# The head of a linear-attention and two-MLP kernel: one load in longer pieces, one pair's rests loaded alone, and a laid-down order between the head's stages

## The chip, the cores and the metric

The kernel runs on one core of a Trainium2 chip. The metric is the device time of one execution in microseconds (us); lower is better. Three runs of the kernel before gave a median of 1557.27 us.

## What is computed

```python
kv  = einsum('bhsd,bhse->bhde', k, v)          # q, k, v: 8 x 8 x 576 x 64, float32
out = einsum('bhsd,bhde->bhse', q, kv)
a   = out / sqrt(mean(out * out, -1) + 1e-6) * g_norm
x   = a.transpose(0, 2, 1, 3).reshape(4608, 512)
h   = x @ moe_w_in                             # 512 x 2048
g   = where(h >= 1, h, where(h <= -1, 0, (h + 1)**2 / 4))
x   = g @ moe_w_out                            # 2048 x 512
h   = x @ moe2_w_in;  r = maximum(h, 0);  out = (r * r) @ moe2_w_out
```

The weights arrive in 64-bit floats and are narrowed on the chip.

## The kernel before

The work goes in three parts: linear attention for eight batches of eight heads, the first MLP and the second. The first MLP's batches 0 to 6 run block by block (16 hidden blocks each), with the attention of the next batch hooked in between; the rest runs in a seven-product form afterwards. The change and the prediction are about the first 75 us only, in which batch 0's attention, the first weights' narrowing and the first MLP blocks overlap.

**Batch 0's attention.** The heads are taken in four pairs (hp 0 to 3). `load_first` starts the loads: of each pair k, v and q as tiles of 128 x 512 on SP's queue, and the last 64 positions of all eight heads (the rests, tiles kvr0 and qr0) on ACT's queue, behind them two copies of g_norm (gvec). `kv_stage` multiplies k by v on TensorE (pkv) and copies the two diagonal blocks to kv0; `t_first` transposes q (pt) and copies it to qT; `o_first` multiplies them (po), takes squares into y on ScalarE and a scaled copy into o, one half of it on VectorE; `r_first` sums the squares over a head (pr), takes Ln and Exp on ScalarE and finishes the norm on VectorE (lines 518, 521 and 522: `newton` and `norm`). Its result t is split into a high and a low part of one input chunk of the MLP: x1_0_0 to x1_0_3, one for each pair, the low part at line 229 on VectorE.

**The weights.** `split_w` takes one block of one weight matrix: a pass on ScalarE (line 267), two on VectorE (lines 269 and 270), a high part by ScalarE (line 216), a low part by VectorE (line 184). Names: w1_0_5 is block 5 of w_in, w1_1_5 block 5 of w_out, d and raw alike.

**The first MLP blocks.** `h_stage` makes hidden block f in PSUM (ph1_0_f, 12 matmuls of 512 columns), ScalarE takes the activation (u1_0_f), and VectorE clamps it at line 706, the last reading of that PSUM bank. Blocks 2 to 5 of batch 0 use the banks acc0 to acc3, in which `out_stage` then gathers the four output sums acc1_0_0 to acc1_0_3:

```python
        pool, tag = (ps_h, "h")
        if (L, b) == (1, 0) and 2 <= f < WAVE:
            pool, tag = (ps_a, f"acc{f - 2}")
```

So acc1_0_3 can begin when the clamp of block 5 has read acc3.

**What sets the order.** The stages are written down by slot numbers (`attention_first`, `SPLITS`, `WARMS`; `keep_warm` puts filler matmuls, pwarm, between them), in slot order, but a scheduling layer places the instructions on each engine's queue by its own costs. `tc.high_priority()` and `tc.issue_after(...)` steer it. Each engine then takes its queue strictly in order.

Of the kernel before, what the change touches and what calls it, by code (L numbers as in the profile page):

```python
# [9 lines left out]
F32 = mybir.dt.float32  # L10
# [66 lines left out]
def linear_attention_rms_two_mlps(  # L77
# [29 lines left out]
    WAVE = 6  # L107
    WHOLE = ((1, 0), (1, 1))
    WARMS = ((0, 5), (6, 5), (8, 3), (12, 4), (14, 3), (20, 3), (26, 3))
    SPLITS = (10, 15, 24, 29, 32, 33)  # L110

    const = ctx.enter_context(tc.tile_pool(name="const", bufs=1))
    wp = ctx.enter_context(tc.tile_pool(name="wp", bufs=1))
# [89 lines left out]
    def engine(op, phase):  # L203
        return engines[next(turns[op][min(phase, 2)])]

    def scaled(e, dst, src, scale):
        if e is nc.scalar:
            e.activation(dst, src, AF.Copy, scale=scale)
        elif e is nc.vector:
            e.tensor_scalar_mul(dst, src, scale)  # L210
        else:
            e.tensor_scalar(dst, src, scale, 0.0, op0=ALU.mult, op1=ALU.add)

    def copy(e, dst, src):
        if e is nc.scalar:
# [11 lines left out]
    def split(t, src, op, phase):  # L227
        hi = copy(engine(op + "_hi", phase), t[:, 0, :], src)
        lo = engine(op + "_lo", phase).tensor_tensor(  # L229
            t[:, 1, :], src, t[:, 0, :].bitcast(F32), ALU.subtract  # L230
        )
        return hi, lo
# [172 lines left out]
    def load_kv(b, hp):  # L405
        h0 = 2 * hp
        if b > 0:

            r = rests[turn[b, hp] % len(rests)]
            kvr[b, hp] = (r[:, 0], r[:, 1])  # L410
        for n, src in enumerate((k, v)):
            pool, tag = (ep, "e") if (b, hp) == (0, NP - 1) else (st, "st")
            t = pool.tile([P, TB], F32, tag=tag, name=f"{'kv'[n]}_{b}_{hp}")
            rows = src[b, h0 : h0 + 2, :TB, :].rearrange("h (p r) d -> p h r d", r=MR)
            if n == 0:

                t = t.rearrange("p (r h d) -> p r h d", h=2, r=MR)
                nc.sync.dma_start(t, rows.rearrange("p h r d -> p r h d"))
            else:
                t = t.rearrange("p (h r d) -> p h r d", h=2, r=MR)  # L420
                nc.sync.dma_start(t, rows)
            kvm.setdefault((b, hp), []).append(t)
            if b > 0:
                rest = src[b, h0 : h0 + 2, TB:, :].rearrange("h p d -> p h d")
                nc.sync.dma_start(kvr[b, hp][n][:REM], rest)
# [14 lines left out]
    def load_first():  # L440


        left = wp.tile([REM, 2, H, D], F32, tag="w0_7", name="kvr0")
        qr = wp.tile([REM, H, D], F32, tag="w1_6", name="qr0")
        for hp in range(NP):
            load_kv(0, hp)
            heads = slice(2 * hp, 2 * hp + 2)
            kvr[0, hp] = (left[:, 0, heads, :], left[:, 1, heads, :])
            pool, tag = (ep, "e") if hp == NP - 1 else (st, "st")
            t = pool.tile([P, TB], F32, tag=tag, name=f"q_0_{hp}")  # L450
            t = t.rearrange("p (c h d) -> p c h d", h=2, c=MR)
            rows = q[0, 2 * hp : 2 * hp + 2, :TB, :].rearrange("h (p c) d -> p c h d", p=P)
            nc.sync.dma_start(t, rows)
            qs[0, hp] = [t[:, c] for c in range(MR)] + [qr[:, heads, :]]
            if hp == 1:
                for f in range(2):
                    load_w(1, f, 0)
            if hp == 0:
                for d, src in ((left[:, 0], k), (left[:, 1], v), (qr, q)):
                    nc.scalar.dma_start(d, src[0, :, TB:, :].rearrange("h p d -> p h d"))  # L460
                for j in range(2):
                    nc.scalar.dma_start(
                        gvec[j * D : (j + 1) * D, :], g_norm.rearrange("(d o) -> d o", o=1)
                    )

    def kv_stage(b, *hps):
        ps = bank(b, f"pkv_{b}_{hps[0]}")
        for n, hp in enumerate(hps):
            kt, vt = kvm.pop((b, hp))
            r = kvr.pop((b, hp))  # L470


            for c in range(MR + 1):
                for j in range(2):
                    s = slice(j * D, (j + 1) * D)
                    d = slice(n * P + j * D, n * P + (j + 1) * D)
                    lhs, rhs = (kt[:, c, j], vt[:, j, c, :]) if c < MR else (r[0][:, j], r[1][:, j])
                    nc.tensor.matmul(ps[s, d], lhs, rhs, start=c == 0, stop=c == MR)  # L478
        for n, hp in enumerate(hps):
            for j in range(2):  # L480
                s = slice(j * D, (j + 1) * D)
                d = slice(n * P + j * D, n * P + (j + 1) * D)
                if b == 0:
                    copy(engine("kv_hi", b), kv0[s, hp, s], ps[s, d])
                    continue
                if (b, hp) in WHOLE:
                    copy(engine("kv_hi", b), kvw[s, hp % 2, s], ps[s, d])
                    continue
                t = kvbd[turn[b, hp] % len(kvbd)]
                copy(engine("kv_hi", b), t[s, 0, s], ps[s, d])  # L490
                nc.vector.tensor_tensor(t[s, 1, s], ps[s, d], t[s, 0, s].bitcast(F32), ALU.subtract)

    def t_first(hp):
        qT = scratch(hp, "qT")
        q5 = qs[0, hp]
        for half in range(2):
            ps = bank(0, f"pt_0_{hp}_{half}")
            for c in range(2):
                nc.tensor.transpose(ps[:, c * P : (c + 1) * P], q5[2 * half + c], ident)
            rest = slice(half * (REM // 2), (half + 1) * (REM // 2))  # L500
            nc.tensor.transpose(ps[:, 2 * P : U], q5[MR][rest], ident[rest, rest])
            copy(engine("q_hi", 0), qT[:, half], ps[:, :U])
        hl[0, hp] = qT

    def o_first(hp):
        qT = hl.pop((0, hp))
        y, o = scratch(hp, "y"), scratch(hp, "o")
        for half in range(2):
            ps = bank(0, f"po_0_{hp}_{half}")
            nc.tensor.matmul(ps[:, :U], kv0[:, hp, :], qT[:, half], start=True, stop=True)  # L510
            nc.scalar.activation(y[:, half], ps[:, :U], AF.Square)
            scaled(engine("o", 0), o[:, half], ps[:, :U], gvec)
        og[0, hp] = (y, o)

# [2 lines left out]

    def norm(t, y, o):  # L520
        nc.vector.scalar_tensor_tensor(t, t, -3.0, y, op0=ALU.add, op1=ALU.mult)
        nc.vector.tensor_tensor(t, o, t, ALU.mult)

    marks = []

    def r_first(hp):
        y, o = og.pop((0, hp))
        t = scratch(hp, "t")
        ms = []
        for half in range(2):  # L530
            ps = bank(0, f"pr_0_{hp}_{half}")
            m = ps[:, :U]
            nc.tensor.matmul(m, ones.bitcast(F32), y[:, half], start=True, stop=True)  # L533
            nc.scalar.activation(y[:, half], m, AF.Ln, bias=lnb, scale=LN_SCALE)
            ms.append(m)
        nc.scalar.activation(y, y, AF.Exp, bias=expb, scale=-0.5)
        square(engine("y", 0), t, y)
        for half in range(2):
            newton(t[:, half], ms[half])
        norm(t, y, o)  # L540
        n = TB // 2
        rem = xrem[0][:, hp, :].rearrange("p (h r) -> p h r", h=2)
        nc.gpsimd.tensor_copy(rem, t[:, :, n:])
        x = xs[1, 0][hp].rearrange("p a (h n) -> p a h n", h=2)
        marks.append(split(x, t[:, :, :n], "x", 0))


    def t_stage(b, hp):
# [86 lines left out]
    def attention_first():  # L635

        slots = {}

        def at(s, f, *a):
            slots.setdefault(s, []).append((f, a))  # L640

        at(0, begin, 0)
        for hp in range(NP):
            at(6 * hp, kv_stage, 0, hp)
            at(6 * hp, t_first, hp)
            at(6 * hp + 8, o_first, hp)
            at(6 * hp + 13, r_first, hp)
        return slots
# [520 lines left out]
    nc.gpsimd.memset(kvw, 0.0)  # L1169
    first = attention_first()  # L1170
    for s, n in WARMS:
        first[s].append((keep_warm, (n,)))
    order = ((0, 0), (1, 0), (2, 0), (3, 0), (4, 0), (0, 1), (1, 1), (5, 0), (2, 1))
    for i, (f, w) in enumerate(order):
        if i < 5:
            first.setdefault(SPLITS[i], []).append((split_w, (1, f, w)))
        else:
            first.setdefault(SPLITS[-1] + 1, []).append((split_later, (1, f, w)))
    for s in sorted(first):
        for f, a in first[s]:  # L1180
            if f in (o_first, r_first):
                with tc.high_priority():
                    f(*a)
            else:
                f(*a)
# [102 lines left out]
```

## Time and profile before

| | |
|---|---|
| median of three runs | 1557.27 us (1557.17 to 1559.74) |
| the profiled execution | 1557.11 us |
| its span, first to last instruction | 1555.3 us |
| TensorE busy | 1546.2 us, 99% |
| VectorE busy | 1133.4 us, 73% |
| ScalarE busy | 973.7 us, 63% |
| chain that ended last | TensorE 97% |

PE is TensorE, DVE is VectorE, ACT is ScalarE; POOL and SP are the two others, of which SP issues most loads. The chain of waits is followed back from the last instruction. A line of the timeline or of the chain gives the start and the length in us, then engine, line of the kernel, operation, and output and input by the program's names without their numbers.

### The profile page before, as it was taken

What the parts mean: (1) busy time and instruction counts of PE and PEld (TensorE: products, weight loads), DVE (VectorE), ACT (ScalarE), POOL (GpSimd) and SP (SyncE); (2) the same over time, 40 slices, a digit from 0 to 9 for tenths busy, and PEclk for the clock granted to TensorE, in tenths of its full rate; (3) what the DMA queues carried; (4) which work ended last, traced back from release to release, by engine and by line L of the source; (5) the groups of instructions that cost most, each with busy time, mean ns of one, the idle gap of its engine ahead of it and who ended that gap; (6) DMA issues with size and microseconds to landing.
All of it is one profiled execution on the core that took longest, in us unless ns stands there. A gap on an engine that the chain in (4) does not pass through costs nothing.

```text
span 1555.3 us, 22355 instructions
## 1 busy us (share of the span) xinstructions
PE 1546.2 (99%) x7729; PEld 1283.6 (83%) x7729; DVE 1133.4 (73%) x2000; ACT 973.7 (63%) x1833; POOL 20.4 (1%) x38
## 2 busy tenths in 40 slices
PE   9999999999999999999999999999999999999999
PEld 5787888888888888888888888888888888888898
DVE  6986886877877776754587558778965596568666
ACT  5977766767666676665565466456646663565374
POOL 0000000000000000000000000000000000000000
PEclk9999999999999999999999999999999999999999
DMA  9666899996878967935676877696876676877796
GB/s 290 194 217 187 274 315 277 309 314 196 275 246 243 281 207 228 295 99 169 196 245 192 224 219 245 194 250 191 258 228 204 203 239 197 242 248 223 214 389 250
DMA packets 327520, 368.23 MB, mean 237 GB/s; under 512 B 196976, under 2 KB 222576, under 8 KB 327408
## 3 DMA queue, kind: packets, MB, share of 16 engines
q1 hardware_dynamic: 295360, 308.60, 66.9%
q10 hardware_dynamic: 32048, 58.20, 9.9%
q8 instruction: 61, 1.00, 0.3%
q14 instruction: 51, 0.42, 0.1%
HBM read 282.59 MB, written 84.15 MB: 236 GB/s over the span
## 4 chain that ended last, share of the span: by engine, by line
PE 97%; ACT 1%; DVE 1%; DMA 1%; issue 0%; DVEq 0%; ACTq 0%
PE po L877 27%; PE ph L877 27%; PE acc L237 19%; PE ph L237 18%; PE po L237 1%; PE pkv L478 1%; PE pr L600 1%; PE pwarm L1150 1%; DMA wf<-wsd 1%; ACT raw L267 0%; ACT w L216 0%; PE pr L533 0%; ACT u L704 0%; DVE t L518 0%; DVE w L184 0%; PE po L510 0%
## 5 line engine op out<-in xcount | busy, mean ns | idle before, releaser
L877 PE MATMUL ph<-x,ws 128*128 128x512 f32 (+1 forms) x2016 | 422.4, 371 | 0.0
L877 PEld LDWEIGHTS ph<-x,ws 128*128 128x128 f32 x2016 | 355.9, 188 | 65.5
L877 PE MATMUL po<-t,ws 128*128 128x512 f32 x1680 | 381.6, 389 | 0.0
L877 PEld LDWEIGHTS po<-t,ws 128*128 128x128 f32 x1680 | 315.4, 188 | 65.4
L237 PE MATMUL ph<-x,w 128*128 128x512 f32 x1344 | 329.3, 392 | 1.3 <-ACT w L216 0.6
L237 PEld LDWEIGHTS ph<-x,w 128*128 128x128 f32 x1344 | 248.8, 188 | 54.0 <-ACT w L216 1.4
L806 DVE TENSOR_TENSOR t<-g,t 128x512 fp32r<-128x512 f32 (+1 forms) x288 | 183.2, 641 | 91.2 <-ACT t L216 84.2
L216 ACT CAST t<-g 128x512 fp32r<-128x512 f32 (+1 forms) x288 | 165.7, 585 | 97.2 <-DVE t L806 50.4
L237 PE MATMUL acc<-gs,w 128*128 128x512 f32 x696 | 173.0, 392 | 1.5 <-DVE u L706 1.5
L237 PE MATMUL acc<-gs,wt 128*128 128x512 f32 x648 | 157.9, 391 | 0.0
L237 PEld LDWEIGHTS acc<-gs,w 128*128 128x128 f32 x696 | 128.6, 188 | 27.8 <-DVE u L706 2.0
L934 DVE TENSOR_TENSOR h<-ph,e 128x512 f32<-128x512 f32 (+1 forms) x144 | 92.7, 645 | 67.4 <-PE ph L877 59.9
L237 PEld LDWEIGHTS acc<-gs,wt 128*128 128x128 f32 x648 | 120.1, 188 | 24.3
L704 ACT ACTIVATE u<-ph,halfb 128x512 f32<-128x512 f32 x112 | 77.3, 690 | 88.7 <-PE ph L237 86.3
L706 DVE SCALAR_TENSOR_TENSOR u<-u,ph 128x512 f32<-128x512 f32 x112 | 76.3, 681 | 54.2 <-ACT u L223 53.8
L941 ACT ACTIVATE h<-h 128x512 f32<-128x512 f32 (+1 forms) x120 | 70.3, 586 | 61.8 <-DVE h L934 57.1
L927 DVE TENSOR_TENSOR e<-ph,e 128x512 f32<-128x512 f32 (+1 forms) x96 | 60.9, 643 | 48.4 <-PE ph L877 47.4
L216 ACT CAST gs<-u 128x512 fp32r<-128x512 f32 x112 | 69.7, 622 | 38.4 <-DVE u L706 35.8
L229 DVE TENSOR_TENSOR gs<-u,gs 128x512 fp32r<-128x512 f32 x112 | 76.8, 686 | 21.7 <-ACT gs L216 21.2
L216 ACT CAST x<-xr 128x512 fp32r<-128x512 f32 (+1 forms) x84 | 49.0, 586 | 40.5 <-DVE xr L857 19.4
L942 ACT ACTIVATE g<-h 128x512 f32<-128x512 f32 (+1 forms) x120 | 70.7, 589 | 3.2
L223 ACT ACTIVATE u<-u 128x512 f32<-128x512 f32 x112 | 70.8, 632 | 1.5 <-ACT u L704 0.6
(134 smaller groups left out, 1531.8 us busy)
## 6 DMA issues: line engine op xcount, KB each, us to landing
ws<-wsd SPq DMA_DIRECT2D x336, 512.0 KB, 4.4
wsd<-s ACTq DMA_DIRECT2D x96, 512.0 KB, 4.9
wt<-wsd SPq DMA_DIRECT2D x54, 512.0 KB, 5.6
raw<-in_moe_w_in_dram SPq DMA_DIRECT2D x32, 512.0 KB, 6.0
raw<-in_moe_w_out_dram SPq DMA_DIRECT2D x32, 512.0 KB, 6.4
xr<-x1d SPq DMA_DIRECT2D x36, 256.0 KB, 4.9
out_dram<-ov SPq DMA_DIRECT2D x142, 64.0 KB, 3.7
wsd<-w SPq DMA_DIRECT2D x17, 512.0 KB, 5.0
```

The costliest lines, as they stand in the source:

```text
L216: return e.copy(dst, src)
L223: e.activation(dst, src, AF.Square)
L229: lo = engine(op + "_lo", phase).tensor_tensor(t[:, 1, :], src, t[:, 0, :].bitcast(F32), ALU.subtract)
L237: nc.tensor.matmul(dst, wt(a), xt(c), start=first and n == 0, stop=last and n == 2)
L704: nc.scalar.activation(u, ps, AF.Relu, bias=halfb, scale=0.5)
L706: nc.vector.scalar_tensor_tensor(u, u, 1.0, ps, op0=ALU.min, op1=ALU.max)
L806: engine2(op + "_lo").tensor_tensor(t[:, 1, :], src, t[:, 0, :].bitcast(F32), ALU.subtract)
L877: nc.tensor.matmul(ps, wt(a), xt(c), start=first and n == 0 and i == 0, stop=last and n == len(lhs) - 1 and i == 2, skip_group_check=True,)
L927: nc.vector.tensor_tensor(e[i, p], bank, e[i, 1], ALU.add)
L934: nc.vector.tensor_tensor(h, bank, add, ALU.add)
L941: nc.scalar.activation(u, h, AF.Relu)
L942: nc.scalar.activation(g, u, AF.Square)
```

## The change

Four edits, all for batch 0 and the first weights. k of batch 0 is loaded as v is, four positions of 64 values in one piece of 1 KB, and `kv_stage` reads it in that layout. The rests of pair 0 (two heads) get transfers of their own, and those of the other six heads follow in three more; gvec comes after these. `SPLITS` moves three of the first narrowing steps to later slots, and pairs 2 and 3 begin eight slots later. And an order is laid down: the first five narrowing steps behind a Ln and an o of certain pairs; products and transposes of pairs 2 and 3 behind the norm of the pair two before and the sum of squares of the pair before; products of pair 1 behind the transposes of pair 0.

```diff
-    SPLITS = (10, 15, 24, 29, 32, 33)
+    SPLITS = (14, 20, 26, 29, 32, 33)
...
-            if n == 0:
+            if n == 0 and b > 0:
 
                 t = t.rearrange("p (r h d) -> p r h d", h=2, r=MR)
                 nc.sync.dma_start(t, rows.rearrange("p h r d -> p r h d"))
...
-            if hp == 0:
-                for d, src in ((left[:, 0], k), (left[:, 1], v), (qr, q)):
-                    nc.scalar.dma_start(d, src[0, :, TB:, :].rearrange("h p d -> p h d"))
+            part = (slice(0, 2), slice(2, H))[min(hp, 1)]
+            for d, src in ((left[:, 0], k), (left[:, 1], v), (qr, q)) if hp < 2 else ():
+                rows = src[0, part, TB:, :].rearrange("h p d -> p h d")
+                nc.scalar.dma_start(d[:, part, :], rows)
+            if hp == 1:
                 for j in range(2):
                     nc.scalar.dma_start(
                         gvec[j * D : (j + 1) * D, :], g_norm.rearrange("(d o) -> d o", o=1)
                     )
...
-                    lhs, rhs = (kt[:, c, j], vt[:, j, c, :]) if c < MR else (r[0][:, j], r[1][:, j])
+                    lhs, rhs = (kt[:, j, c] if b == 0 else kt[:, c, j], vt[:, j, c, :]) if c < MR else (r[0][:, j], r[1][:, j])
...
         for hp in range(NP):
-            at(6 * hp, kv_stage, 0, hp)
-            at(6 * hp, t_first, hp)
+            at(6 * hp + 8 * (hp > 1), kv_stage, 0, hp)
+            at(6 * hp + 8 * (hp > 1), t_first, hp)
             at(6 * hp + 8, o_first, hp)
             at(6 * hp + 13, r_first, hp)
...
+    scales, logs, splits = [], [], []
     for s in sorted(first):
         for f, a in first[s]:
             if f in (o_first, r_first):
                 with tc.high_priority():
+                    r = f(*a)
+                (logs if f is r_first else scales).append(r)
+            elif f is split_w and len(splits) < 5:
+                splits.append(a)
+                i = (0, 1, 2, 2, 3)[len(splits) - 1]
+                with tc.issue_after(logs[i].ins), tc.issue_after(scales[i].ins):
+                    f(*a)
+            elif f in (t_first, kv_stage) and a[-1] > 1:
+                with tc.issue_after(normed[a[-1] - 2].ins), tc.issue_after(summed[a[-1] - 1].ins):
+                    f(*a)
+            elif f is t_first:
+                turned = f(*a)
+            elif f is kv_stage and a[1] > 0:
+                with tc.issue_after(turned.ins):
                     f(*a)
             else:
                 f(*a)
```

The helpers return their last instruction for this: `t_first` its last transpose, `o_first` its scaled copy (`scales`), `r_first` its last Ln (`logs`), `norm` its last multiplication (`normed`), and `summed` holds the last sum of squares. Line numbers of the changed kernel are a little higher: the clamp of line 706 is at 712, `kv_stage`'s product of 478 at 480, pt at 501 and 503, po at 513, pr at 537, pwarm at 1156.

The built order shows the change in three places. TensorE's queue behind the products of pair 1, before:

```order
L510 MATMUL po_0_0_0_284<-qT_0_0_235,kv0_126 128x288
L510 MATMUL po_0_0_1_288<-qT_0_0_235,kv0_126 128x288
L533 MATMUL pr_0_0_0_333<-y_0_0_282,ones_121 128x288
L499 MATMUL pt_0_1_0_266<-ident_120,q_0_1_149 128x128 x2
L533 MATMUL pr_0_0_1_336<-y_0_0_282,ones_121 128x288
L501 MATMUL pt_0_1_0_266<-ident_120,qr0_133 128x32
```

and in the change:

```order
L501 MATMUL pt_0_1_0_269<-ident_120,q_0_1_147 128x128
L513 MATMUL po_0_0_0_287<-qT_0_0_238,kv0_126 128x288
L513 MATMUL po_0_0_1_291<-qT_0_0_238,kv0_126 128x288
L501 MATMUL pt_0_1_0_269<-ident_120,q_0_1_147 128x128
L503 MATMUL pt_0_1_0_269<-ident_120,qr0_133 128x32
L501 MATMUL pt_0_1_1_274<-ident_120,q_0_1_147 128x128 x2
L503 MATMUL pt_0_1_1_274<-ident_120,qr0_133 128x32
L1156 LDWEIGHTS warm_188
L1156 MATMUL pwarm_295<-warm_188 128x512
L1156 LDWEIGHTS warm_188
L1156 MATMUL pwarm_295<-warm_188 128x512
L537 MATMUL pr_0_0_1_308<-y_0_0_285,ones_121 128x288
```

All six transposes of pair 1 and two filler matmuls now come ahead of the first reduction of pair 0; two more fillers and the reduction of the other half follow.

VectorE's queue up to the clamp of block 5 (u1_0_5), before:

```order
L269 TENSOR_SCALAR d1_1_5_677<-raw1_1_5_520 128x512
L706 SCALAR_TENSOR_TENSOR u1_0_3_696<-u1_0_3_696,ph1_0_3_683 128x512
L270 SCALAR_TENSOR_TENSOR d1_1_5_677<-raw1_1_5_520,d1_1_5_677 128x512
L706 SCALAR_TENSOR_TENSOR u1_0_4_780<-u1_0_4_780,ph1_0_4_767 128x512
L184 TENSOR_TENSOR w1_1_5_680<-d1_1_5_677,w1_1_5_680 128x2x256
L706 SCALAR_TENSOR_TENSOR u1_0_5_817<-u1_0_5_817,ph1_0_5_804 128x512
```

and in the change, the last twelve rows:

```order
L270 SCALAR_TENSOR_TENSOR d1_0_8_668<-raw1_0_8_619,d1_0_8_668 128x512
L270 SCALAR_TENSOR_TENSOR d1_1_6_764<-raw1_1_6_593,d1_1_6_764 128x512
L269 TENSOR_SCALAR d1_1_7_800<-raw1_1_7_635 128x512
L184 TENSOR_TENSOR w1_0_8_671<-d1_0_8_668,w1_0_8_671 128x2x256
L269 TENSOR_SCALAR d1_0_9_727<-raw1_0_9_665 128x512
L270 SCALAR_TENSOR_TENSOR d1_1_7_800<-raw1_1_7_635,d1_1_7_800 128x512
L270 SCALAR_TENSOR_TENSOR d1_0_9_727<-raw1_0_9_665,d1_0_9_727 128x512
L184 TENSOR_TENSOR w1_1_6_767<-d1_1_6_764,w1_1_6_767 128x2x256
L184 TENSOR_TENSOR w1_1_7_803<-d1_1_7_800,w1_1_7_803 128x2x256
L184 TENSOR_TENSOR w1_0_9_730<-d1_0_9_727,w1_0_9_730 128x2x256
L269 TENSOR_SCALAR d1_0_10_791<-raw1_0_10_724 128x512
L712 SCALAR_TENSOR_TENSOR u1_0_5_820<-u1_0_5_820,ph1_0_5_807 128x512
```

The narrowing of blocks 6 to 9 has moved ahead of that clamp. The low part of x1_0_3 is VectorE's 62nd row in both; the clamp is 34 instructions behind it before and 56 in the change.

TensorE's queue up to the output sum acc1_0_3, before:

```order
L237 MATMUL acc1_0_1_849<-gs1_0_0_587,w1_1_0_494 128x512 x3
L237 MATMUL acc1_0_1_849<-gs1_0_1_625,w1_1_1_501 128x512
L237 MATMUL acc1_0_2_850<-gs1_0_0_587,w1_1_0_494 128x512 x3
L237 MATMUL acc1_0_1_849<-gs1_0_1_625,w1_1_1_501 128x512 x2
L237 MATMUL acc1_0_2_850<-gs1_0_1_625,w1_1_1_501 128x512 x3
L237 MATMUL acc1_0_3_851<-gs1_0_0_587,w1_1_0_494 128x512 x3
```

and in the change:

```order
L574 MATMUL po_1_1_0_824<-qT_1_1_748,kvw_218 128x288
L574 MATMUL po_1_1_1_837<-qT_1_1_748,kvw_218 128x288
L237 MATMUL ph1_0_7_979<-x1_0_0_220,w1_0_7_625 128x512 x2
L237 MATMUL acc1_0_2_853<-gs1_0_0_590,w1_1_0_497 128x512 x3
L237 MATMUL acc1_0_2_853<-gs1_0_1_628,w1_1_1_504 128x512 x3
L237 MATMUL acc1_0_2_853<-gs1_0_2_674,w1_1_2_518 128x512 x3
L606 MATMUL pr_1_1_0_953<-wk0_1_1_746,ones_121 128x288
L606 MATMUL pr_1_1_1_956<-wk0_1_1_746,ones_121 128x288
L237 MATMUL ph1_0_7_979<-x1_0_0_220,w1_0_7_625 128x512
L237 MATMUL ph1_0_7_979<-x1_0_1_221,w1_0_7_625 128x512 x3
L237 MATMUL ph1_0_7_979<-x1_0_2_222,w1_0_7_625 128x512 x3
L237 MATMUL ph1_0_7_979<-x1_0_3_223,w1_0_7_625 128x512 x3
```

after which its next row is the first of acc1_0_3. Hidden block 7, the po and pr of batch 1's pair 1 and a third term of each output sum stand ahead of it now.

## Rows read from the trace of the kernel before

**Rows 1.** Waits of TensorE, 0 to 125 us: total us, times, longest us.
```profile
PE acc L237 <- DVE u L706: 1.5, 1, 1.5
...
PE pr L533 <- DVE t L518: 0.9, 1, 0.9
PE ph L237 <- ACT w L216: 0.6, 2, 0.4
PE ph L237 <- DVE kv L218: 0.4, 1, 0.4
```

**Rows 2.** Waits of TensorE, 125 to 1556 us.
```profile
PE po L237 <- DVE qT L559: 0.3, 1, 0.3
```

**Rows 3.** Timeline of VectorE: start us, length us, engine, line, operation.
```profile
10.60 0.15 DVE L1163 TENSOR_SCALAR gvec<-gvec 128x1 f32<-128x1 f32 x1
...
16.90 0.52 DVE L210 TENSOR_SCALAR o<-po,gvec 128x288 f32<-128x288 f32 x1 [0.98 <-ACT y L511]
...
39.50 0.68 DVE L229 TENSOR_TENSOR x<-t,x 128x512 fp32r<-128x512 f32 x1
40.10 0.75 DVE L269 TENSOR_SCALAR d<-raw 128x512 int32<-128x512 int32 x2
...
59.43 0.69 DVE L706 SCALAR_TENSOR_TENSOR u<-u,ph 128x512 f32<-128x512 f32 x1 [0.23 <-ACT u L223]
```

**Rows 4.** Windows: us, busy of PE, PEld, DVE, ACT, POOL, PEclk, DMA share, GB/s.
```profile
5.00:10.00 5.00, 5.00 (x38) 2.33 (x36) 0.26 (x1) 0.00 (x0) 0.00 (x0) 1.00 1.19 284
...
25.00:30.00 5.00, 4.57 (x20) 2.81 (x19) 4.21 (x11) 3.35 (x7) 0.51 (x1) 1.00 1.05 397
```

**Rows 5.** Chain of waits, first 15 us: start us, length us, what.
```profile
1.19 4.88 PE pwarm L1150 x11
...
9.31 0.22 PE pt L499 x2
...
10.25 0.88 PE pkv L478 x20
11.13 1.17 PE po L510 x4
...
13.28 0.49 PE pr L533 x2
...
14.49 0.75 PE pwarm L1150 x3
```

**Rows 6.** Timeline of ScalarE and its DMA issues (ACTq).
```profile
1.55 0.90 ACTq L460 DMA_DIRECT2D kvr<-in_v_dram  x1
...
13.10 0.50 ACT L534 ACTIVATE y<-pr,lnb 128x288 f32<-128x288 f32 x1 [0.15 <-PE pr L533]
...
14.58 0.78 ACT L536 ACTIVATE y<-y,expb 128x576 f32<-128x576 f32 x1
15.76 0.41 ACT L511 ACTIVATE y<-po 128x288 f32<-128x288 f32 x1 [0.40 <-PE po L510]
```

**Rows 7.** Groups of VectorE by shape, 0 to 140 us: busy us, mean ns.
```profile
L184 DVE TENSOR_TENSOR w<-d,w 128x512 fp32r<-128x512 f32 x32 | 21.8, 685 | 2.8 <-ACT w L216 2.5
L270 DVE SCALAR_TENSOR_TENSOR d<-raw,d 128x512 int32<-128x512 int32 x32 | 21.6, 685 | 1.7 <-ACT raw L267 1.3
L269 DVE TENSOR_SCALAR d<-raw 128x512 int32<-128x512 int32 x32 | 13.2, 419 | 0.0
...
L518 DVE SCALAR_TENSOR_TENSOR t<-pr,t 128x288 f32<-128x288 f32 x16 | 6.7, 449 | 0.8 <-ACT t L223 0.7
...
L521 DVE SCALAR_TENSOR_TENSOR t<-t,wk 128x576 f32<-128x576 f32 x4 | 3.0, 750 | 0.0
```

**Rows 8.** Chain of waits, 51 to 76 us.
```profile
53.96 0.96 PE acc L237 x3
...
62.46 3.18 PE acc L237 x13
65.64 0.97 PE po L568 x4
```

More of the change, by code (lines that the diff above doesn't have):

```diff
@@ L207, in scaled @@
         if e is nc.scalar:
-            e.activation(dst, src, AF.Copy, scale=scale)
+            return e.activation(dst, src, AF.Copy, scale=scale)
         elif e is nc.vector:
-            e.tensor_scalar_mul(dst, src, scale)
+            return e.tensor_scalar_mul(dst, src, scale)
         else:
-            e.tensor_scalar(dst, src, scale, 0.0, op0=ALU.mult, op1=ALU.add)
+            return e.tensor_scalar(dst, src, scale, 0.0, op0=ALU.mult, op1=ALU.add)
     def copy(e, dst, src):
@@ L500, in t_first @@
             rest = slice(half * (REM // 2), (half + 1) * (REM // 2))
-            nc.tensor.transpose(ps[:, 2 * P : U], q5[MR][rest], ident[rest, rest])
+            last = nc.tensor.transpose(ps[:, 2 * P : U], q5[MR][rest], ident[rest, rest])
             copy(engine("q_hi", 0), qT[:, half], ps[:, :U])
         hl[0, hp] = qT
+        return last
     def o_first(hp):
@@ L511, in o_first @@
             nc.scalar.activation(y[:, half], ps[:, :U], AF.Square)
-            scaled(engine("o", 0), o[:, half], ps[:, :U], gvec)
+            last = scaled(engine("o", 0), o[:, half], ps[:, :U], gvec)
         og[0, hp] = (y, o)
+        return last
     def newton(t, m):
@@ L521, in norm @@
         nc.vector.scalar_tensor_tensor(t, t, -3.0, y, op0=ALU.add, op1=ALU.mult)
-        nc.vector.tensor_tensor(t, o, t, ALU.mult)
-    marks = []
+        return nc.vector.tensor_tensor(t, o, t, ALU.mult)
+    marks, normed, summed = [], [], []
     def r_first(hp):
@@ L532, in r_first @@
             m = ps[:, :U]
-            nc.tensor.matmul(m, ones.bitcast(F32), y[:, half], start=True, stop=True)
-            nc.scalar.activation(y[:, half], m, AF.Ln, bias=lnb, scale=LN_SCALE)
+            total = nc.tensor.matmul(m, ones.bitcast(F32), y[:, half], start=True, stop=True)
+            last = nc.scalar.activation(y[:, half], m, AF.Ln, bias=lnb, scale=LN_SCALE)
             ms.append(m)
@@ L539, in r_first @@
             newton(t[:, half], ms[half])
-        norm(t, y, o)
+        summed.append(total)
+        normed.append(norm(t, y, o))
         n = TB // 2
@@ L545, in r_first @@
         marks.append(split(x, t[:, :, :n], "x", 0))
+        return last
     def t_stage(b, hp):
@@ L1171, in linear_attention_rms_two_mlps @@
     for s, n in WARMS:
-        first[s].append((keep_warm, (n,)))
+        first.setdefault(s, []).append((keep_warm, (n,)))
     order = ((0, 0), (1, 0), (2, 0), (3, 0), (4, 0), (0, 1), (1, 1), (5, 0), (2, 1))
```

## The prediction

> **What bounds the kernel now.** I read the waits of TensorE first, once for the first 125 us and once for the rest. TensorE is busy 99% of the span. In the first 125 us it stands for 1.5 us before the first output matmul and for 0.9, 0.6 and 0.4 us in shorter waits [rows 1]; after 125 us it waits once, for 0.3 us [rows 2]. So what the change can give or take lies in the head. Every microsecond by which TensorE is held back there stays in the total, since nothing later has slack to return it. None of these waits ends with a transfer: VectorE or ScalarE ends each. That is the second thing to see: the head is paced by the order in which those two work through their queues. In VectorE's own order of time, the low part of the last of batch 0's four input chunks (x1_0_3) starts at 39.50 us, and the clamp of hidden block 5 (u1_0_5) starts at 59.43 us [rows 3]. That clamp matters because it is the last reader of PSUM bank acc3, which the output sum acc1_0_3 needs next.
>
> **1-KB pieces.** The four k loads of batch 0 change from 1024 pieces of 256 B to 256 pieces of 1 KB. The trace doesn't show this load in the new shape; the nearest rows are the stretch in which 256-B pieces prevail, 284 GB/s, and one with mostly 1-KB and 4-KB pieces, 397 GB/s [rows 4]. A k of 0.262 MB takes 0.92 us at the one and 0.66 us at the other: 0.26 us less for each, 1.05 us for four. On the path I cost it at nothing: the first pair's products wait behind eleven warm-up matmuls that start at 1.19 us and last 4.88 us, and from there to the transposes at 9.31 us TensorE does the same work in a new order, so pair 1's products still start near 10.25 us [rows 5]. If that cover were gone, the gain would be at most the 1.05 us. The Trainium skill, page "DMA: Bandwidth & Descriptors", section Specifications, puts line rate at 512 B and more and says that shorter pieces are read, modified and written; by that rule the edit helps, and if transfers set the head, the time would be that of the third rival below.
>
> **The first pair's rests by own transfers.** ACT's queue gets three more DMAs before the two for gvec, and one of them waits until the first q has landed. An issue there takes up to 0.90 us [rows 6], so gvec can come up to 2.7 us later; VectorE takes it now at 10.60 us without a wait [rows 3]. Its first reader on ScalarE stands behind the first y, which can end at 12.3 us at the earliest (11.13 plus 0.16 for the one transpose moved ahead, a sixth of the 0.94 below, about 0.6 for the first po, half of 1.17, and some 0.4 for y). So the cost lies between nothing and 1.0 us; I take nothing, as it needs more than 1.6 us of delay. ScalarE has no work yet while it issues. SP's queue keeps its order, and POOL's four small copies follow the chunks, with nobody waiting for them here.
>
> **The order between the pairs.** On TensorE the six transposes of pair 1 and two pairs of warm-up matmuls now stand ahead of pair 0's reductions pr. From the end of pair 1's products at 11.13: po 1.17, the six transposes 0.94 (9.31 to 10.25), two warm-up matmuls 0.50 (three took 0.75), one pr 0.49 [rows 5], together 14.23 us. So pair 0's Ln starts at 14.25 instead of 13.10. From there to its Exp, with one weight pass between, is 1.48 us now, and from Exp to pair 1's Square 0.70 when nothing else holds it (0.78 less 0.08 of overlap) [rows 6]: Exp 15.73, Square 16.43 instead of 15.76. From that Square to VectorE's o of pair 1 is 1.14 us (15.76 to 16.90) [rows 3, 6]: 17.6 instead of 16.90, **0.7 us later**.
>
> From there to the low part of x1_0_3 VectorE has the same 42 instructions in both orders and one more, the first pass of weight block 1: 22.60 us (16.90 to 39.50) plus 0.42 less 0.08. The overlap of 0.08 is seen where an instruction of 0.68 us at 39.50 is followed by one at 40.10 [rows 3]. Pairs 2 and 3 now come later relative to the first weights: their copies of kv and qT stand behind pair 1's chain on VectorE, so TensorE waits for them, an estimated 2.6 us near 22.5, and some ScalarE casts that VectorE needs come behind that. Waits that go are replaced by these; I take 0.4 us more in all, between 0 and 0.8. x1_0_3 then starts at 17.6 + 22.60 + 0.34 + 0.4 = 40.9 us, **1.4 us later**.
>
> **The clamp of block 5.** This is the largest term, and only the built order shows it. From x1_0_3 to the clamp VectorE has 34 instructions before and 56 in the changed order: the same 34 and 22 more, drawn ahead of it. They are four of pair 0 of batch 1 (two of 0.45 and two of 0.75), its transposition (as wide, taken at 0.75) and chunk (0.68), eleven passes of weight narrowing (six of 0.42, five of 0.685) and five low parts (0.685) [rows 7]: 2.40 + 0.75 + 0.68 + 5.95 + 3.43 = 13.2, less 22 times 0.08 of overlap, 11.45 us. VectorE is full there, so they count whole. The clamp starts at 40.9 + 19.93 (39.50 to 59.43) + 11.45 = 72.3 and ends at 73.0; acc1_0_3 starts at 73.05.
>
> What TensorE has done by then: in the changed order 123 matmuls of 512 columns stand ahead of acc1_0_3 (blocks 0 to 7 and 27 of the output), po and pr of pair 1 of batch 1 among them. Before, 84 were done at the wait that ends at 53.96, and 36 more, of which the first and last lines are shown, by 65.64; with the po of 0.97 behind them, three more matmuls (13 took 3.18, so 0.73) and a pr of the same width as that po, 0.97, it is 68.3 us [rows 8]. **TensorE is 4.75 us behind** at this point, some 3 us of it in one wait. Weight blocks 7 to 9 are narrowed sooner for it, which may return up to the 0.6 us that TensorE waits on such casts now [rows 1]; I take 0.25.
>
> **Sum:** +4.75 - 0.25 = **+4.5 us**. The profiled execution took 1557.11 us (span 1555.3 and 1.8 around it), 0.16 below the median of 1557.27. That gives 1561.6 us. Bounds of the unknown terms: chunk on time and all 0.6 returned +2.7; gvec late and more waits +6.2.
>
> **Rivals.** (1) *The early narrowing pays back* (no change that can be measured; 0.2%, or 3.1 us, is about what a measurement of this kernel can tell from none). For it: blocks 7 to 9 come early and transfers are faster. If x1_0_3 starts at 39.50 as now and VectorE's waits shrink by another 1 us, it is 4.75 - 1.4 - 1 - 0.6 = +1.75, 1558.9 us. Against it: TensorE's later waits are only 0.3 us, so little is left to return. (2) *The clock drops.* The warm-up matmuls took 0.44 us each at first (4.88 for eleven) and 0.25 later [rows 5], the 1.2 and the 2.4 GHz level. The granted clock stays up with a wait of 1.5 us in it; the new waits of an estimated 2.6 and 3 us are longer. Some 3 us of work at the lower level would cost 3 us more: +7.5, 1564.6 us. (3) *Transfers set the head* (faster). Then the k's 1.05 us and the earlier rests move every stage forward. The point from which it decides: the clamp must end by 68.3, so x1_0_3 must start at 36.2 or sooner, 3.3 us before now. Below that TensorE's waits in the head can go, 3.4 us in all [rows 1]: 1553.7 us. Against it: no wait there ends with a transfer, and the pieces alone give a third of the 3.3. (4) *The order isn't what runs*: the built order shows that it is, so this has no chance of its own.
>
> **Numbers.** My forecast 0.66, rival 1 0.19, rival 2 0.09, rival 3 0.06. Slower by over 0.2%: most of the forecast (0.64, since its lower bound falls under 3.1) and rival 2, 0.73. Within: rival 1 and the rest of the forecast, 0.21. Faster: rival 3, 0.06. The range leaves out rival 3, the lowest part of rival 1 and the highest of rival 2: 1558.4 to 1565.2.
>
> **What would show it.** In the new trace the low part of x1_0_3 near 41 us; the clamp of block 5 near 72 us with 55 instructions between; a TensorE wait of about 3 us before acc1_0_3 that VectorE's L712 ends; a wait of 2 to 3 us before po of pair 2. If that clamp comes before 68 us, or if TensorE doesn't wait for it, the forecast is wrong; if matmuls near 25 us take twice their time, rival 2 is at work; if pair 1's products start well before 10 us, the third.

## The result and the profile after

| | median us | lowest to highest | ratio to the kernel before |
|---|---|---|---|
| kernel before | 1557.11 (6 runs) | 1556.26 to 1559.74 | |
| changed kernel | 1569.32 (6 runs) | 1565.86 to 1571.15 | 1.0074 [1.0061, 1.0087] |

The change makes the kernel slower by 12.2 us (0.74%, interval 0.61 to 0.87%). The forecast was slower by 4.5, 1561.6 us, with an upper bound of 1565.2. The profiled execution took 1569.1 us, its span 1567.3, 12.0 more than before.

The first view is again the waits of TensorE (total us, times, longest us), 0 to 125 us, which answers to [rows 1]:

```profile
PE acc L237 <- DVE u L712: 3.1, 2, 2.6
PE po L513 <- DVE qT L218: 2.6, 1, 2.6
PE pr L537 <- DVE qT L218: 1.5, 1, 1.5
...
PE ph L237 <- ACT w L216: 0.6, 1, 0.6
```

and after 125 us, which answers to [rows 2]:

```profile
PE po L237 <- ACT qT L216: 2.6, 3, 1.2
```

Two of the long waits are those that were forecast: 2.6 us before the third pair's output matmuls (po of pair 2) and 2.6 before acc1_0_3. Two were not: 1.5 us before the first sums of squares (pr), and three waits after 125 us that come to 2.6, where before there was one of 0.3.

The second thing is in the windows of five us (busy us of PE, PEld, DVE, ACT, POOL; granted clock; DMA share; GB/s). Before, the clock stood at 1.00, as in [rows 4]. After:

```profile
10.00:15.00 5.00, 3.31 (x17) 2.04 (x15) 1.88 (x8) 1.21 (x3) 0.00 (x0) 0.93 1.13 341
15.00:20.00 5.00, 5.00 (x16) 2.97 (x15) 1.38 (x4) 3.69 (x8) 0.00 (x0) 0.72 1.12 365
...
25.00:30.00 5.00, 2.98 (x7) 1.58 (x8) 4.20 (x10) 2.71 (x6) 0.24 (x1) 0.80 1.04 410
30.00:35.00 5.00, 5.00 (x36) 3.35 (x36) 3.79 (x10) 3.68 (x9) 0.00 (x0) 0.86 1.01 262
...
75.00:80.00 5.00, 4.29 (x12) 3.40 (x13) 4.52 (x9) 2.92 (x6) 0.00 (x0) 0.66 0.94 311
```

The granted clock falls three times. In windows of one us (only the clock's column is told here) it stands at 0.67, 0.50, 0.50 and 0.62 from 14 to 18 us, so that 0.33 + 0.50 + 0.50 + 0.38 = 1.71 us of full-speed work is lost; the stretches from 28 and from 76 us look the same. Three of them make 5.1 us. TensorE's timeline (start us, length us, then the instruction, and in brackets its wait) has each fall behind a wait:

```profile
1.19 3.97 PE L1156 MATMUL pwarm<-warm 128*128 128x512 bf16 x11 [1.19 <-DVE warm L1151]
...
9.16 0.69 PE L480 MATMUL pkv<-v,k 128*64 128x64 f32 x16
...
14.26 1.22 PE L537 MATMUL pr<-y,ones 128*128 128x288 f32 x2 [1.54 <-DVE qT L218]
...
16.12 1.17 PE L537 MATMUL pr<-y,ones 128*128 128x288 f32 x2
...
19.04 0.70 PE L537 MATMUL pr<-y,ones 128*128 128x288 f32 x2
...
27.02 1.37 PE L513 MATMUL po<-qT,kv 128*128 128x288 f32 x4 [2.56 <-DVE qT L218]
...
75.70 4.85 PE L237 MATMUL acc<-gs,w 128*128 128x512 f32 x13 [2.59 <-DVE u L712]
```

A pair of pr takes 1.17 us in the low stretch and 0.70 behind it; the thirteen matmuls of the sums take 4.85 us where thirteen took 3.18 before [rows 8]. **Waits and clock together are the loss, to within a microsecond:** TensorE's idle time between matmuls, added over its whole trace, grew from 4.2 to 11.3 us, 7.1 more, and 5.1 for the clock makes 12.2, against 12.0 in the span. Against it stands a gain at the start: the same eleven warm-up matmuls took 3.97 us here and 4.88 before [rows 5], 0.9 less, so that 0.7 us of the loss stays without a name. This is a ledger and no list of causes: where TensorE waits for another engine later on, work that was slowed ahead of that wait need not have cost time.

VectorE's timeline says where the waits come from; it answers to [rows 3]:

```profile
13.10 0.15 DVE L1169 TENSOR_SCALAR gvec<-gvec 128x1 f32<-128x1 f32 x1 [3.06 <-DMA gvec<-in_g_norm_dram]
13.17 0.45 DVE L218 COPY kv<-pkv 64x64 f32<-64x64 f32 x2
13.65 0.46 DVE L218 COPY qT<-pt 128x288 f32<-128x288 f32 x1
...
19.65 0.52 DVE L210 TENSOR_SCALAR o<-po,gvec 128x288 f32<-128x288 f32 x1 [2.37 <-ACT y L514]
...
25.47 0.74 DVE L526 TENSOR_TENSOR t<-o,t 128x576 f32<-128x576 f32 x1
26.24 0.23 DVE L218 COPY kv<-pkv 64x64 f32<-64x64 f32 x1
26.50 0.82 DVE L218 COPY qT<-pt 128x288 f32<-128x288 f32 x2
...
43.94 0.69 DVE L229 TENSOR_TENSOR x<-t,x 128x512 fp32r<-128x512 f32 x1 [0.69 <-ACT x L216]
...
74.97 0.68 DVE L712 SCALAR_TENSOR_TENSOR u<-u,ph 128x512 f32<-128x512 f32 x1
```

Three places matter. VectorE stands for 3.06 us before the small scaling of gvec, and pair 1's copies of kv and qT are queued behind it. The wait of 1.54 us is put down to that qT copy, which ends at 14.11. But ScalarE is held by gvec as well: its scaled copy o waits 1.99 us for it, and the second half of the squares y, which the first of the sums reads, is queued behind it and ends at 14.09:

```profile
13.29 0.50 ACT L208 ACTIVATE o<-po,gvec 128x288 f32<-128x288 f32 x1 [1.99 <-DVE gvec L1169]
13.69 0.40 ACT L514 ACTIVATE y<-po 128x288 f32<-128x288 f32 x1
```

So gvec holds the sums on two ways that end within 0.02 us of each other, and no run parts them. The second place: the copies of pair 2 (26.24 and 26.50) stand behind the norm of pair 1 (25.47), as the change's order has it. And the third: the clamp of block 5 starts at 74.97, 31.03 us behind the low part of x1_0_3 at 43.94.

### The profile page after: what moved, and what is told of

Its sections match the earlier page's. It is cut to its first block, busy times and chain, and to the rows that moved or that the text cites. A ratio compares the mean times of both kernels' runs of the same rounds, so it can differ in the third digit from the quotient of the medians.

```text
span 1567.3 us, 22316 instructions
## 1 busy us (share of the span) xinstructions
PE 1551.3 (99%) x7727; PEld 1286.3 (82%) x7729; DVE 1135.8 (72%) x2000; ACT 973.5 (62%) x1833; POOL 13.8 (1%) x38
## 4 chain that ended last, share of the span: by engine, by line
PE 67%; DVE 0%; ACT 0%; issue 0%
PE po L883 27%; PE ph L883 27%; PE acc L237 7%; PE ph L237 6%; PE po L237 0%; PE pkv L480 0%; PE pr L606 0%; DVE qf L563 0%; ACT qT L216 0%; DVE ov L1015 0%; DVE u L712 0%
```

## Experiments

Eleven kernels ran in three sets (1 to 4, 5 to 8, then 9 to 11 and number 4 once more), each set beside the kernel before, which took 1557.51, 1557.12 and 1557.29 us (19, 25 and 33 runs).

**1. gvec ahead of the other heads' rests.** All else as in the changed kernel.

```diff
-            if hp == 1:
+            if hp == 0:
                 for j in range(2):
                     nc.scalar.dma_start(
```

> Changed kernel with one edit: gvec's two DMAs stand behind the rests of the first pair and ahead of those of the other six heads. Theory G (gvec is late): VectorE takes gvec by 10.5 us and not at 13.10, its 3.06 us of idle time ahead of gvec goes, and with it TensorE's wait of 1.54 us at 14.26 and the stretch at half clock behind it (14.3 to 17.7, worth 1.7 us): about 1566 us. Rival O (the order of the stages decides alone): the time lost there is lost at the next wait anyway, the time stays within 1 us of the changed kernel's 1569.

Measured: 1565.67 us, ratio 1.0051 [1.0036, 1.0066]; 3.6 us under the changed kernel. VectorE's timeline:

```profile
9.48 0.15 DVE L1169 TENSOR_SCALAR gvec<-gvec 128x1 f32<-128x1 f32 x1 [7.31 <-DMA gvec<-in_g_norm_dram]
...
17.41 0.52 DVE L210 TENSOR_SCALAR o<-po,gvec 128x288 f32<-128x288 f32 x1 [1.49 <-ACT y L514]
...
41.37 0.69 DVE L229 TENSOR_TENSOR x<-t,x 128x512 fp32r<-128x512 f32 x1 [0.69 <-ACT x L216]
...
72.40 0.68 DVE L712 SCALAR_TENSOR_TENSOR u<-u,ph 128x512 f32<-128x512 f32 x1
```

gvec is taken at 9.48, the wait of 1.54 us and the first low stretch are gone, and these places come 2.2 to 2.6 us earlier (o of pair 1 from 19.65 to 17.41, the clamp from 74.97 to 72.40). TensorE comes to acc1_0_3 earlier by as much, after a wait as long:

```profile
73.14 3.24 PE L237 MATMUL acc<-gs,w 128*128 128x512 f32 x13 [2.58 <-DVE u L712]
```

Theory G holds; rival O falls. In the traces the order on TensorE and on ScalarE is the same as in the changed kernel from end to end, and on VectorE all but the first copies, where gvec's scaling now stands ahead of pair 0's. So this is the late transfer with its place among those copies, and nothing else.

**2. Both load edits under the old order.** Kernel of before with:

```diff
-            if n == 0:
+            if n == 0 and b > 0:
...
-            if hp == 0:
-                for d, src in ((left[:, 0], k), (left[:, 1], v), (qr, q)):
-                    nc.scalar.dma_start(d, src[0, :, TB:, :].rearrange("h p d -> p h d"))
+            part = (slice(0, 2), slice(2, H))[min(hp, 1)]
+            for d, src in ((left[:, 0], k), (left[:, 1], v), (qr, q)) if hp < 2 else ():
+                rows = src[0, part, TB:, :].rearrange("h p d -> p h d")
+                nc.scalar.dma_start(d[:, part, :], rows)
+            if hp == 1:
```

> Kernel of before with both load edits (k in 1-KB pieces, the first pair's rests by own transfers with gvec behind the second three) and none of the order between stages. Theory G: gvec is taken near 13 us here too and holds VectorE's copies of the second pair; the first matmuls start 1 us earlier, but TensorE waits 1 to 2 us near 14 us, perhaps with a stretch at half clock: 1558 to 1561 us. Rival O: the loads are harmless, 1556 to 1557.5 us.

Measured: 1556.45 us, 0.9996 [0.9986, 1.0005]. The expectation of theory G missed here: gvec is taken at 14.53 us, later than in the changed kernel, and the kernel is no slower than the one before. In this built order VectorE stands only 1.46 us before gvec, and TensorE has other work of the first two pairs ahead of the sums in its queue. So a late gvec costs much less with the old order than with the new one; experiment 11 asks whether it costs nothing.

**3. The order alone.** The changed kernel with both load edits undone (the diff of experiment 2 the other way round).

> Changed kernel with both load edits undone (k in 256-B pieces, all rests and then gvec with the first pair), so the order between the stages alone. Theory G with the order's own losses: no wait of 1.5 us near 14 us; the waits of about 2.6 us before the output matmuls of the third pair and before acc1_0_3 stay, each with a stretch of some 3.4 us at half clock: 4.5 + 3.4 = 8 us more than before, 1565 us, plus up to 2.5 in waits after 240 us. Rival O: like the changed kernel, 1568 to 1570 us. Rival L (the loads cost the most): under 1562 us.

Measured: 1565.09 us, 1.0049 [1.0034, 1.0064], as theory G's sum had it, with other parts: one wait of 4.6 us instead of two of 2.6.

```profile
PE po L511 <- DVE qT L218: 4.6, 1, 4.6
PE ph L237 <- ACT w L216: 3.2, 2, 1.8
```

The low stretch behind the 4.6 us is twice as long as the others (clock low until 33 us). The order alone loses 7.6 us; the new loads, harmless under the old order, make the new one 4.2 us worse, and most of that is gvec's place: with it mended, experiment 1 takes 1565.67 us, about as long as the order alone.

**4. The 1-KB pieces alone.** Kernel of before with the first two lines of the diff of experiment 2 and `kt[:, j, c]` for batch 0. It was run twice.

> Kernel of before with one edit: the first batch's k in 1-KB pieces. If the transfers set the first products (in the changed kernel they start 1 us earlier), the first qT copy comes near 8.8 us instead of 9.74 and up to 1 us is won: 1556 to 1556.5 us. As predicted at first (warm-up matmuls cover it): 1557.1 us, no change.

> The kernel of before with k in 1-KB pieces once more, in five rounds, for its interval: between 1556 and 1556.6 us, 0.5 to 1.2 us under the kernel of before, if the first measurement holds; within 0.3 us of before if it was chance.

Measured: 1556.28 us, 0.9991 [0.9981, 1.0000], and 1556.12 us, 0.9994 [0.9985, 1.0003]. Some 1.2 us are won, at the edge of what can be told. The expected place was not the one: the built order of the head changed with this edit too, and VectorE's timeline shows kv's copies ahead of qT's, and gvec held back here as well:

```profile
8.89 0.46 DVE L218 COPY kv<-pkv 64x64 f32<-64x64 f32 x2 [6.72 <-PE pkv L478]
11.41 0.46 DVE L218 COPY qT<-pt 128x288 f32<-128x288 f32 x1 [2.06 <-PE pt L501]
12.80 0.15 DVE L1163 TENSOR_SCALAR gvec<-gvec 128x1 f32<-128x1 f32 x1 [0.94 <-DMA gvec<-in_g_norm_dram]
```

An edit of a load's shape alone thus moves instructions on the engines. How much of the 1.2 us is the transfers' and how much the new order's is not shown.

**5. No order between the pairs.** The changed kernel without:

```diff
-            at(6 * hp + 8 * (hp > 1), kv_stage, 0, hp)
-            at(6 * hp + 8 * (hp > 1), t_first, hp)
+            at(6 * hp, kv_stage, 0, hp)
+            at(6 * hp, t_first, hp)
...
-            elif f in (t_first, kv_stage) and a[-1] > 1:
-                with tc.issue_after(normed[a[-1] - 2].ins), tc.issue_after(summed[a[-1] - 1].ins):
-                    f(*a)
-            elif f is t_first:
-                turned = f(*a)
-            elif f is kv_stage and a[1] > 0:
-                with tc.issue_after(turned.ins):
-                    f(*a)
```

> Changed kernel without the order between the pairs' stages (slots of the third and fourth pair as before, no rule that their k and q stages come after the norms and sums of earlier pairs); the loads, the narrowing's places and its rules stay. Theory P (the pairs' rule is what costs): the wait of 2.6 us before the third pair's output matmuls goes with its stretch at half clock, the low part of x1_0_3 starts before 39 us, the clamp of block 5 before 64, no wait of 2.6 us before acc1_0_3: 1555.5 to 1559 us. Rival S (the narrowing's rule costs): still above 1563 us.

Measured: 1557.86 us, 1.0005 [0.9995, 1.0014]: 11.5 of the 12.2 us are back, as theory P had it. TensorE's waits:

```profile
PE ph L237 <- ACT w L216: 1.6, 2, 0.8
...
PE pkv L480 <- DMA kvr<-in_v_dram: 0.7, 1, 0.7
```

The third pair's wait, the one before acc1_0_3 and all after 125 us are gone; the clock stays at 1.00 in this profile (five of the ten runs have a mean of 0.997 to 0.999); x1_0_3 starts at 38.88 and the clamp at 62.36. The order of the narrowing steps and the late gvec (14.06) are still in this kernel; they cost no more than the loads win.

**6. No order on the narrowing.** The changed kernel with `SPLITS` as before and without the branch for `split_w`.

```diff
-    SPLITS = (14, 20, 26, 29, 32, 33)
+    SPLITS = (10, 15, 24, 29, 32, 33)
...
-            elif f is split_w and len(splits) < 5:
-                splits.append(a)
-                i = (0, 1, 2, 2, 3)[len(splits) - 1]
-                with tc.issue_after(logs[i].ins), tc.issue_after(scales[i].ins):
-                    f(*a)
```

> Changed kernel without the order laid on the first weights' narrowing (SPLITS and their rules as before); loads and the pairs' rules stay. Theory P: the wait of about 2.6 us before the third pair's output matmuls stays, with 1.7 us for the stretch at half clock behind it; whether the clamp of block 5 comes late is the question: with it 1565 us, without it 1560 to 1562 us. Rival S: 1556 to 1558 us.

Measured: 1561.49 us, 1.0026 [1.0017, 1.0036]. The third pair's wait stays at 2.7 us with its low stretch; the clamp of block 5 comes at 65.07, 22.5 us behind x1_0_3 instead of 31.0, and TensorE does not wait for it (it waits 1.4 us at 77 us for another step of VectorE's). Theory P holds again, and the time is the one that it gave for a clamp that isn't waited for: the pairs' order makes the first wait by itself, and both orders together put the narrowing ahead of the clamp.

**7. Filler matmuls in two of the waits.** The changed kernel with

```diff
-    WARMS = ((0, 5), (6, 5), (8, 3), (12, 4), (14, 3), (20, 3), (26, 3))
+    WARMS = ((0, 5), (6, 5), (8, 9), (12, 4), (14, 14), (20, 3), (26, 3))
```

> Changed kernel with 6 more warm-up matmuls ahead of the first pair's sums and 11 more ahead of the third pair's output matmuls, 0.216 us each (1.3 and 2.4 us of work into waits of 1.54 and 2.57 us). Theory K (half of the unexpected loss is the clock): no stretch at half clock before 40 us; that returns 3.4 us, less what the longer queue and the replanned order cost (an estimated 1.3): about 1567 us. Rival W (only the waits cost, the clock's fall is covered by the wait for VectorE that follows): 1569 to 1571 us.

Measured: 1568.55 us, 1.0071 [1.0056, 1.0086], between the two expectations, and it tells nothing apart. The fillers changed the built order, and the waits they were to fill came later and stayed:

```profile
PE po L513 <- DVE qT L218: 1.8, 1, 1.8
PE pr L537 <- DVE qT L218: 1.7, 1, 1.7
```

Behind both the clock fell, and once more behind a wait of 2.3 us near 506 us. The clock's price was therefore not isolated by an experiment. What bears on it are the runs of one program that differ in nothing else: of the changed kernel's six, the one with a mean granted clock of 1.000 took 1565.86 us, the five with 0.996 to 0.998 took 1567.80 to 1571.15. A loss of 0.003 of 1567 us would be 4.7. It is a comparison of six runs, of which only the first has a trace.

**8. The later blocks' narrowing behind the clamp.** The changed kernel with

```diff
+    def split_last(*a):
+        with tc.issue_after(clamps[0, WAVE - 1].ins):
+            split_w(*a)
...
+            late = 0 < i < WAVE - 1 and i + at > 6 - w
             if i + at < NF:
-                hook(2 * i + w, later, 1, i + at, w)
+                hook(2 * (WAVE - 1) + w if late else 2 * i + w, split_last if late else later, 1, i + at, w)
```

where `clamps` holds the clamps of line 712.

> Changed kernel with one edit: the narrowing of the first weights from block 7 on (second weights from block 6 on) that is hooked into the first wave stands behind the clamp of hidden block 5. Theory C (the clamp is late because narrowing stands ahead of it): the clamp starts near 66 us and not at 74.97, the wait of 2.59 us before acc1_0_3 goes, and 2.5 to 5 us are won: 1564 to 1567 us. Rival N (the late narrowing is then waited for by blocks 7 to 9): the wait moves to these blocks and the time stays at 1568 to 1570 us.

Measured: 1562.30 us, 1.0030 [1.0021, 1.0040], 7.0 us under the changed kernel and better than theory C had it. VectorE's timeline has the clamp at 67.10, 22.1 us behind x1_0_3 (44.99) instead of 31.0:

```profile
67.10 0.68 DVE L712 SCALAR_TENSOR_TENSOR u<-u,ph 128x512 f32<-128x512 f32 x1
```

and TensorE's waits, first before 125 us and then after, are

```profile
PE po L513 <- DVE qT L218: 2.6, 1, 2.6
PE pr L537 <- DVE qT L218: 1.7, 1, 1.7
...
PE acc L237 <- DVE u L712: 0.5, 1, 0.5
```

```profile
PE po L237 <- DVE qT L565: 1.1, 1, 1.1
PE po L237 <- ACT qT L216: 0.2, 1, 0.2
```

The wait before acc1_0_3 is gone with its low stretch, blocks 7 to 9 wait for nothing in its place (rival N falls), and the waits after 125 us shrink from 2.6 to 1.3. That is 2.6 + 1.7 + 1.3 = 5.6 of the 7.0.

**9. Both mends together**, the edits of experiments 1 and 8.

> Changed kernel with both mends: gvec's DMAs ahead of the other heads' rests, and the later blocks' narrowing behind the clamp of block 5. If the two losses add (3.6 us won by the first alone, 7.0 by the second alone), 1569.3 - 10.6 = 1558.7 us, with the wait of 2.6 us before the third pair's output matmuls left and a stretch at half clock behind it. If the second mend already took what gvec's lateness costs, 1561 to 1562.5 us.

Measured: 1558.88 us, 1.0012 [1.0004, 1.0021]. The two losses add, to 0.2 us. What is left over the kernel before, 1.6 us, holds the third pair's wait (2.6, with a low stretch behind it); what returns the rest of that was not taken apart.

**10 and 11. Can gvec's place win something under the old order?** First, the kernel of before with 1-KB pieces and gvec issued first of all on ACT's queue:

```diff
+        for j in range(2):
+            nc.scalar.dma_start(gvec[j * D : (j + 1) * D, :], g_norm.rearrange("(d o) -> d o", o=1))
         for hp in range(NP):
             load_kv(0, hp)
```

> Kernel of before with k in 1-KB pieces and gvec's two DMAs issued first of all on ACT's queue. If gvec, taken at 12.80 us with the pieces alone, holds the head there, it is now taken without a wait and another 0.5 to 1 us is won: 1555.3 to 1555.8 us. If the order of the engines' work decides, or the rests now come 1.2 us late, 1556.3 to 1557.5 us.

Measured: 1557.83 us, 1.0005 [0.9996, 1.0013]. gvec no longer holds anything, but a larger load does:

```profile
PE pkv L476 <- DMA v<-in_v_dram: 2.5, 1, 2.5
```

and the clock falls to 0.50 from 12 to 14 us. Then, the kernel of experiment 2 with gvec between pair 0's rests and those of the other heads (the edit of experiment 1):

> Kernel of before with both load edits and gvec ahead of the other heads' rests. Loads with gvec late took 1556.45 us; if gvec's lateness cost anything under the old order, 1555.5 us or less; if nothing, 1556 to 1557 us.

Measured: **1555.29 us, 0.9986 [0.9977, 0.9995]**. This is the fastest kernel of the study, 2.0 us under the kernel before and 14.0 under the changed one. By its expectation (1555.5 or less) a late gvec does cost something under the old order: each beside the kernel before of its own set, experiment 2 won 1.1 us and this one 2.0. Their intervals overlap, so the 0.9 us between them is a hint and no more. Its waits in the head:

```profile
PE pkv L480 <- DMA v<-in_v_dram: 1.7, 1, 1.7
PE pwarm L1152 <- DVE warm L1147: 1.2, 1, 1.2
PE pr L602 <- ACT wk L208: 0.4, 1, 0.4
```

gvec is taken at 8.00 us. The largest wait is now one for a transfer, and it lies in the first ten us; the wait of 1.5 us before the first output matmul [rows 1] is not there any more.

## Why the prediction was half right

**The order between the pairs and the clamp: right in mechanism and size.** Experiment 1 shows these steps without gvec's lateness. Forecast and measured there: o of pair 1 at 17.6 and 17.41; x1_0_3 at 40.9 and 41.37; the clamp at 72.3 and 72.40; acc1_0_3 at 73.05 and 73.14. In the changed kernel itself the clamp follows x1_0_3 by 31.03 us where 19.93 + 11.45 = 31.38 were worked out. Experiment 8 confirms the cause: with 17 fewer instructions between (39 from x1_0_3 to the clamp instead of 56), the wait goes. So the built order, priced with durations from the trace, gave the largest term well. One part is luck: in experiment 1 the warm-up matmuls took 3.91 us instead of 4.88, and pair 1's products then waited 0.38 us and a transpose behind them 0.40 us for transfers; the one nearly made up for the other, so that po started at 11.10 where the prediction had 11.13.

**gvec "at nothing": the first step that failed.** The prediction had gvec up to 2.7 us late (it came 2.5 late) and looked at its first reader on ScalarE, with a slack of 1.6 us. That slack was not there: the first y ended at 11.30 us and not at 12.3 or later, for the whole start ran earlier, and ScalarE waited 1.99 us, twice the upper bound of 1.0. And the prediction did not look at what stands behind gvec's own scaling on VectorE: two copies of kv and the qT copies of pair 1, which came as late. Measured: acc1_0_3 at 75.70 instead of 73.14, 2.6 us, and 3.6 us in the median (experiment 1). Experiments 2 and 11 add that the same lateness costs at most about 1 us in the old order, so its price could only be read from the new one.

**The clock: a rival that came true, with too small a chance.** Rival 2 had 0.09 and one stretch that costs 3 us; there were three that cost 1.7 each, and its sign, matmuls near 25 us at twice their time, came true (from 28 us). The prediction argued that the clock stayed up with a wait of 1.5 us in it [rows 1]; in the changed kernel a wait of the same 1.54 us was followed by the low level, and so were both of 2.6. With 1.7 us for the stretch behind it, a wait of 2.6 us cost up to 4.3; the experiments don't isolate how much of it. This should have been part of the forecast: the prediction itself had two waits of an estimated 2.6 and 3 us, longer than any in the trace of before.

**"Nothing later": the third step that failed.** The sum ended at acc1_0_3, since TensorE waits only 0.3 us after 125 us [rows 2]. But the scheduling layer planned the rest anew too: TensorE's order differs in the traces up to 601 us, in the attention of batch 6, and three waits for qT appeared, at 268, 312 and 506 us. One of them on ScalarE's timeline:

```profile
310.64 0.62 ACT L216 CAST s<-s 128x512 fp32r<-128x512 f32 x1 [2.21 <-DMA wsd<-s]
311.17 0.68 ACT L710 ACTIVATE u<-ph,halfb 128x512 f32<-128x512 f32 x1
311.75 0.66 ACT L216 CAST qT<-qf 128x576 fp32r<-128x576 f32 x1
```

The cast of qT, for which TensorE waits, stands behind one that waits 2.21 us for a transfer, in which narrowed weights go out to be kept for later. This costs 2.6 - 0.3 = 2.3 us, and it is the most fickle part: the waits for qT come to 2.8, 1.3 and 0.9 us in experiments 1, 8 and 9. In experiment 1 the first of them, of 1.53 us, has a stretch at half clock behind it (0.50 from 267 to 270 us), which the changed kernel's profile does not have there:

```profile
265.00 0.40 PE L237 MATMUL po<-qT,kvbd 128*128 128x288 f32 x1 [1.53 <-ACT qT L216]
```

The sum as it should have been, in the profiled executions: 7.4 us behind at acc1_0_3 (75.70 against 68.3: the forecast 4.75, gvec's 2.6 with its low stretch in it), 1.7 for the stretch behind it, 2.3 for the later waits: 11.4 of 12.0. The 0.25 that early narrowing was to return did not show.

**The 1-KB pieces: put at nothing, and the head's traces bear it out.** The prediction had warm-up matmuls cover the loads, so that pair 1's products still start near 10.25 us [rows 5], and products well before 10 us were to be the sign of its third rival, in which transfers set the head. In the changed kernel they start at 9.16. But that is the warm-up matmuls' pace and not the loads: from the end of the eleven to the products it is 4.00 us there (5.16 to 9.16) and 4.18 before (6.07 to 10.25). In experiments 7 and 8, with the same loads and the same head, the eleven took 4.67 and 4.50 us and the products started at 9.87 and 9.70, again 4.01 behind. So the sign came true without the rival. Alone the edit wins some 1.2 us (experiment 4), at the edge of what can be told and with a built order that differs. The Trainium skill, page "DMA: Bandwidth & Descriptors", section Specifications, puts line rate at pieces of 512 B and more. These traces agree in sign: the first load of k took 3.6 us from issue to landing before and 2.8 in experiment 4.

## What to carry to other kernels

When a small transfer is moved back in a queue, look at the instruction that takes it and at what that engine has queued behind it, as well as at who reads its result and how early that reader can be ready. Where a scheduling layer plans the whole program, an edit at the head, even a load's new shape, plans the rest anew: read the built order as far as it differs, and test a mend by itself before laying down more rules. And price a new wait of TensorE with the low clock that can follow it.

## What the runs showed of the hardware that was not expected

- Waits of the same length did not always lower the clock. 1.54 us did so in the changed kernel and not in the kernel before, 1.75 did in experiment 8, and 1.61 and 1.74 did not in experiments 2 and 11. 2.59 us before acc1_0_3 did so in the profile of the changed kernel (0.66 from 75 to 80 us), and 2.58 in that of experiment 1 did not, where thirteen matmuls behind it took 3.24 us and the clock stayed at 1.00. What decides is not shown. The wait of the kernel before, and its window from 50 to 55 us with the clock at 1.00:

```profile
53.96 0.96 PE L237 MATMUL acc<-gs,w 128*128 128x512 f32 x3 [1.54 <-DVE u L706]
```

```profile
50.00:55.00 5.00, 3.46 (x14) 2.43 (x15) 4.93 (x9) 4.97 (x10) 0.00 (x0) 1.00 1.06 385
```

- The same eleven warm-up matmuls at the start took from 3.91 us (experiment 1) to 4.88 (kernel before, experiments 3, 4 and 5); experiment 4's kernel, run twice, has 4.88 and 4.74. So one profile's times in the head can lie up to 1 us beside another's for this alone. The column of the granted clock has 1.00 from 0 to 5 us in the kernel before and in the changed one, so this is read from the matmuls' pace.
- The runs of a program with such waits spread more: 5.3 us over six runs of the changed kernel, 1.65 over eleven of the fastest one, whose mean granted clock was 1.000 in each.
- In experiment 4 the first weights' loads on SP's queue were issued at 5.44 us instead of 7.47, and gvec's two issues on ACT's queue, on which nothing had moved, began at 5.92 us instead of 4.34 and took 2.44 us instead of 1.71. gvec was taken at 12.80 instead of 10.60 [rows 3]. So a small transfer came later though nothing ahead of it on its own queue had moved; whether the earlier loads on the other queue held it back is not shown.
